# Two more units of an expert layer by nested Strassen products, with their transposed sums turned by DMA and VectorE

## Chip, cores and metric

The kernel runs on one core of a Trainium2 chip. The metric is the device time of one execution in microseconds, as the median over runs. The engines are TensorE (PE in the profile, its weight loads PEld), VectorE (DVE), ScalarE (ACT), GpSimd (POOL) and SyncE (SP, whose queue issues most DMAs).

## The reference

All data are float32. The attention comes first, and its output, as 3072 tokens by 512 features, is the input of the expert layer. The change lies in the expert layer's second product.

```python
# attention: q, k, v (4, 8, 768, 64), lam (8,); blocks of 64 positions
for b in range(nb):
    intra = einsum('bhij,bhjd->bhid', einsum('bhic,bhjc->bhij', qb, kb) * Dmask, vb)
    inter = einsum('bhid,bhde->bhie', qb * lam_pow, kv_state)
    out[:, :, sl] = intra + inter
    kv_state = lam_block * kv_state + einsum('bhsd,bhse->bhde', kb * rev_pow, vb)
x = out.transpose(0, 2, 1, 3).reshape(3072, 512)
# experts: w1 (4, 512, 1024), w2 (4, 1024, 512), domain_probs (3072, 4)
p = domain_probs / (domain_probs.sum(-1, keepdims=True) + 1e-09)
for e in range(4):
    h = maximum(x @ w1[e], 0.0)
    out += p[:, e:e + 1] * (h @ w2[e])
```

## The kernel before

**Units.** The 3072 tokens are cut into three groups of 1024 (g = 0, 1, 2; `LAST` is 2). A unit is one group with one expert: `units` has twelve, 0 to 3 for group 0, 4 to 7 for group 1, 8 to 11 for group 2, experts in the order 0, 1, 2, 3. The main loop takes unit after unit and in each the seven products of one Strassen level (`M1` to `M7`). Into each of these it interleaves the second product of the present unit with the first product of the next (`ahead`). So one pass of a unit is seven products of eight steps each; a step is a few matmuls, and the counter `now[0]` counts steps.

**First product** (`first_product`, L974). Two Strassen levels: seven times seven products of 128 by 128 weights with 256 tokens, two matmuls each. Its output blocks `m` are hidden values, hidden features on partitions and tokens along the row. DVE adds each result out of PSUM to a block; ACT copies or applies the ReLU (L982, L986, L915).

**Second product, plain** (`second_product`, L1028), for groups 0 and 1: one Strassen level, 112 matmuls of the program in a unit. The hidden block is the stationary operand, so the result has tokens on partitions. DVE multiplies it with the gate, which is there one number per partition, and adds it into `acc` (L1046, L1042). After the last expert the rows go to the output. The weights come by `feed2` from `w2_sums` or from the input.

**Second product, nested** (`nested_product`, L1256), for group 2: two levels, 98 matmuls in a unit. Here the weight block is stationary and the result is transposed, output features on partitions and tokens along the row; it stays so in `sums`, one tile for each of the seven products, over all four experts. The gate is now a row: `gated` multiplies the hidden block on POOL with a gate that a DMA has spread over the partitions (`gate_bc`). `outer_sums` makes the four outer sums of hidden blocks: ACT copies a block into a PSUM bank (`bring`, L838, tile `hp`), and DVE subtracts out of it into `hT`. `inner_sums` makes the inner sums on POOL (tile `acc` or `hT`). In the last unit the seven `sums` are joined, turned to token rows by TensorE (`give`, `turn_end`) or by DVE in 32 by 32 blocks (`give_across`), and stored. The last unit's `PLAIN` product uses one level (L1191).

**Weights of the nested product.** `prepare_w2_ops(e)` loads `w2[e]` (`w2b`), makes outer and inner sums of it on POOL (`w2o`, `ops`) and stores seven operands to DRAM (`w2_ops`). It runs as "chores": closures that `pump` takes one at a time as a modelled POOL (`busy`, with 480 elements of a row per step) comes free. `store` puts the DMAs of a finished chore into a queue; `until` forces chores whose result is needed. Before, expert e's is prepared while unit 4 + e runs. `feed3` loads the operands, two inner ones at a time, into the six buffers of `w2t`.

**Order.** All engines' queues are written out by hand: what a step appends stands in each engine's queue in that order. `background` holds DVE work and `aside` POOL work; a step takes one of each. `attention(g)` places the next groups' attention at steps given by `BEGIN`, eight chunks a fixed number of steps apart, and `x_fill` reads its result back as operands of the first product. All elementwise work goes through the helper `tt`, so that its line is L102 for DVE and POOL alike, and the tile names tell the groups apart. All DMAs that the text speaks of, but for the gates, are issued from SP's queue.

Of the kernel before, what the change touches and what calls it, by code (L numbers as in the profile page):

```python
# [21 lines left out]
def kernel(  # L22
# [78 lines left out]
    def tt(eng, o, a, b, op):  # L101
        eng.tensor_tensor(out=o, in0=a, in1=b, op=op)  # L102
        if eng is nc.gpsimd:
            busy[0] = max(busy[0], now[0]) + math.prod(o.shape[1:]) / 480
        else:
            vector(math.prod(o.shape[1:]), PSUM in (a.space, b.space))
# [6 lines left out]
    now, busy, free, filled = [0], [0.0], [0.0], [0.0]  # L113
# [7 lines left out]
    LAST = NG - 1  # L121

# [56 lines left out]
    def pump(pace=1.0, force=False):  # L179
        all_added(None if force else now[0])  # L180
        while results:
            results.pop(0)()
        while late and (force or late[0][0] <= now[0]):
            late.pop(0)[1]()
        begins = chores and (force or free[0] <= now[0])
        while queue and (force or queue[0][0] <= now[0] or begins and len(queue) > LEFT):
            queue.pop(0)[1]()
        if begins:
            begin = free[0] = max(free[0], now[0] - 1)
            was = max(busy[0], now[0])  # L190
            chores.pop(0)()
            free[0] = max(free[0], begin + max(pace * (busy[0] - was), 1))
# [106 lines left out]
    def inner_w2(e, m, blk):  # L299
        b = {f"A{i + 1}{j + 1}": blk[:, j, :, i * P:(i + 1) * P] for i in range(2) for j in range(2)}  # L300
        s = stage.tile([P, 4, 2, P], FP32, name="ops", tag="st")
        for name, x, y, op in S_OPS:
            b[name] = s[:, SLOT[name]]
            tt(nc.gpsimd, b[name], b[x], b[y], op)
        to = w2_ops[e, MS.index(m)]
        store(lambda: (
            nc.sync.dma_start(out=to[:, 0], in_=b["A11"]),
            nc.sync.dma_start(out=to[:, 1:3], in_=s[:, 0:2]),
            nc.sync.dma_start(out=to[:, 3], in_=b["A22"]),
            nc.sync.dma_start(out=to[:, 4], in_=b["S1"]),  # L310
            nc.sync.dma_start(out=to[:, 5], in_=b["A12"]),
            nc.sync.dma_start(out=to[:, 6], in_=b["S4"]),
            made.add(("w2", e, m)),
        ))

    def prepare_w2_ops(e):
        st = {}

        def block(name, i, j):
            t = stage.tile([P, 2, 2, DH], FP32, name="w2b", tag="st")  # L320
            src = moe_w2[e, j * W:(j + 1) * W, i * DH:(i + 1) * DH]
            nc.sync.dma_start(out=t[:].rearrange("p q c d -> p (q c) d"), in_=src.rearrange("(k p) d -> p k d", p=P))
            st[name] = t

        def total(name, a, b, op):
            t = stage.tile([P, 2, 2, DH], FP32, name="w2o", tag="st")
            halves(*(x[:].rearrange("p q c d -> p q (c d)") for x in (t, st[a], st[b])), op)
            st[name] = t

        return weight_steps(block, total, lambda m: inner_w2(e, m, st[A_OF[m]]))  # L330
# [164 lines left out]
    last_gate = consts.tile([P, CPG * E], FP32, name="last_gate")  # L495


    gate_rows = dram.tile([CPG, E, P], FP32, name="gate_rows")
    gate_bc = decay[:]

    def gates():
# [8 lines left out]
        for i in range(CPG):  # L510
            t = token(LAST, i // 4, i % 4) // P
            nc.vector.tensor_copy(out=last_gate[:, i * E:(i + 1) * E], in_=gate[:, t])

    def turn_gates():
        p, o = bank("s0", "gp"), small("gr")
        n = CPG * E
        nc.tensor.transpose(out=p[0:n, 0:P], in_=last_gate[:], identity=ident[:])
        nc.scalar.copy(out=o[0:n, 0:P], in_=p[0:n, 0:P])
        nc.scalar.dma_start(out=gate_rows[:].rearrange("n e p -> (n e) p"), in_=o[0:n, 0:P])
# [231 lines left out]
    BEGIN = {1: (24, 13), 2: (8 * 19, 22)}  # L751
    steps = []

    def attention(g):
# [4 lines left out]
        for i in range(CPG):  # L759
# [8 lines left out]
            if n == 2 * CPG + 3:  # L768
                put(s + 17, turn_gates)
# [41 lines left out]
    outer = {e: {n: {} for n in ("B11", "B12", "B21", "B22", "T1", "T2", "T3", "T4")} for e in range(E)}  # L811
# [43 lines left out]
    EARLY = E - 1, "M3"  # L855
# [42 lines left out]
    def finished(g, e, m, blocks, new):  # L898

        def later(to, a, b, order, relu=False):  # L900
# [7 lines left out]
            def step(at):  # L908
                x = there[at]
                if g == LAST and at != order[-1]:  # L910
                    bring(order[order.index(at) + 1])
                o = to[at] if at in to else small("m" + at)
                tt(nc.vector, o[:], x[:], b[at][:], ALU.add)
                if relu:
                    nc.scalar.activation(out=o[:], in_=o[:], func=AF.Relu)  # L915
                    if g == LAST:
                        gated(e, 1, 1, at, o)
# [4 lines left out]
            if g == LAST:  # L922
                background.append(lambda: bring(order[0]))
            background.extend(lambda at=at: step(at) for at in order)

        def keep(c, i, j):
            if g == LAST:
                outer_sums(e, *{(0, 1): (("T1",), ("T3", "T2")), (1, 0): (("T4",),)}.get((i, j), ()))
# [21 lines left out]
    def first_product(g, e, m, blocks, tags):  # L950
# [16 lines left out]
        def inner(i):  # L967
# [17 lines left out]
            if m in OUT and (at == "12" or not begins):  # L985
                nc.scalar.activation(out=new[at][:], in_=new[at][:], func=AF.Relu)  # L986
                if g == LAST:
                    gated(e, *OUT[m], at, new[at])
# [24 lines left out]
    def second_product(g, e, m, banks):  # L1013

        def part(sj, s):
# [31 lines left out]
            if e == E - 1 and m in ("M2", "M6", "M5", "M3"):  # L1047
                results.append(lambda: nc.sync.dma_start(out=rows[n][:, j * DH:(j + 1) * DH], in_=o))
# [10 lines left out]

    SEQ3 = ("M1", "M3", "M5", "M7", "M6", "M2", "M4")  # L1060
# [3 lines left out]
    def feed3(e, m, k):  # L1064

        until(("w2", e, m))
        if e == E - 1 and m != SEQ3[0]:

            if k == 0:
                t = xp.tile([P, 7, 256], FP32, name="w2s", tag="x" + SEQ[SEQ3.index(m)])  # L1070
                if (e, m) == PLAIN:
                    i, j = int(A_OF[m][1]) - 1, int(A_OF[m][2]) - 1
                    src = moe_w2[e, j * W:(j + 1) * W, i * DH:(i + 1) * DH]
# [3 lines left out]
                nc.sync.dma_start(out=t[:], in_=w2_ops[e, MS.index(m)].rearrange("p k c d -> p k (c d)"))  # L1077
# [6 lines left out]
            out=t[:, 0:n], in_=w2_ops[e, MS.index(m), :, 2 * k:2 * k + n].rearrange("p k c d -> p k (c d)"),  # L1084
# [97 lines left out]
    PLAIN = E - 1, "M2"  # L1182
# [23 lines left out]
    END = E - 1, SEQ3[-1]  # L1206
# [28 lines left out]

    def nested_product(e, m, tags):
        if e == 0:
# [8 lines left out]
        def inner(x, i):  # L1246
# [16 lines left out]
            if begins and e == 0:  # L1263
# [7 lines left out]
        def done():  # L1271
            if e == E - 1:
                to_join(m)

# [178 lines left out]
    units = [(g, e) for g in range(NG) for e in range(E)]  # L1453
    fill = [(*u, m) for u in units[2:] for m in SEQ]
    fill2 = [(*u, m) for u in units[:-E] for m in SEQ2]
# [51 lines left out]
    fill3 = [(e, m, k) for e in range(E) for m in SEQ3 for k in range(4)]  # L1507
# [6 lines left out]
    PACE = 1.0, 1.4, 1.0  # L1514
    for at, (g, e) in enumerate(units):
# [3 lines left out]
        nested, nests = g == LAST, ahead and ahead[0] == LAST  # L1519
        if g == LAST - 1:  # L1520
            chores.extend(prepare_w2_ops(e))
        if at == 6:
            forget()
        blocks, banks = {}, {}
        for i in range(7):
            if fill2:
                feed2(*fill2.pop(0))
            if (g, e) < (LAST, 0):
# [5 lines left out]
            if nests and i == 2:  # L1534
                nc.scalar.dma_start(
                    out=gate_bc, in_=gate_rows[:, ahead[1]].partition_broadcast(P),
                )
            if nested:
                pair = (at * 7 + i) % 2 if ahead else i % 3
                b = nested_product(e, SEQ3[i], (("q01", "q02"), ("q11", "q12"), ("g1", "g3"))[pair])  # L1540
                if i < 6 and (e, SEQ3[i + 1]) != PLAIN:
                    inner_sums(e, SEQ3[i + 1])
            else:
                b = second_product(g, e, SEQ2[i], banks)
            if nests and i == 6:
                inner_sums(ahead[1], SEQ3[0], nested)
                if ahead[1] == EARLY[0]:
# [4 lines left out]
            if nested and (e, SEQ3[i]) == END:  # L1552
# [9 lines left out]
            for x, part in enumerate(order):  # L1562
# [15 lines left out]
                if nested or nests:  # L1578
                    take(aside)
                if nested and ahead and x in (1, 3) and fill3:  # L1580
# [47 lines left out]
```

## Time and profile before

| | before |
|---|---|
| runs shown | 1170.91, 1176.38, 1176.42 us (median 1176.38) |
| profiled execution | 1171.55 us, its span 1169.8 us |
| PE busy, weight loads busy | 1157.8 us (99%), 1006.5 us (86%) |
| DVE, ACT, POOL busy | 791.7, 271.1, 646.1 us |
| granted PE clock | 1.0 throughout |
| DMA | 255.63 MB moved, mean 219 GB/s |

The span goes from the first to the last instruction; 1.75 us of the execution lie around it. The attention of group 0 and the start take the first 86 us, then come the units: plain ones to about 864 us, where the first nested product starts, and nested ones to the end. A trace row of a 128x256 matmul counts two for each matmul of the program. In the groups of the profile the form `out<-in` gives tile names, then shapes, the count, the sum and mean of the busy time, and the idle time just before with what ended it.

### The profile page before, as it was taken

Reading aid. Unit: us, or ns where it says so; the run is one execution under the profiler, and the core shown is the slowest. Engines: PE = TensorE matmul, PEld = TensorE weight load, DVE = VectorE, ACT = ScalarE, POOL = GpSimd, SP = SyncE. Lnnn points to the kernel's source line nnn. Section 1 sums busy time; section 2 is a strip of 40 time slices with the busy share of each in tenths; the row PEclk is TensorE's granted clock in tenths of the full one; section 3 lists DMA queues with packets and bytes.
Section 4 is the critical chain, followed back from the end, with each engine's and each line's share of the span. In section 5 each row is a group of like instructions: output and inputs, shape, how many; then the busy total and the mean of one; then the engine's idle time right before and its main releaser. Section 6 shows DMA issues by size and latency. Waiting matters only on the chain.

```text
span 1169.8 us, 21185 instructions
## 1 busy us (share of the span) xinstructions
PE 1157.8 (99%) x8095; PEld 1006.5 (86%) x8095; DVE 791.7 (68%) x1407; ACT 271.1 (23%) x540; POOL 646.1 (55%) x640
## 2 busy tenths in 40 slices
PE   8999999999999999999999999999999999999998
PEld 7888888888888888888888888888888888888887
DVE  4666895578478567657747836745775666777785
ACT  4321122112211201211211120221233342341231
POOL 2846327546655761065245215655893683882884
PEclk9999999999999999999999999999999999999999
DMA  9884668998997996787868757785765445354442
GB/s 208 219 257 153 185 195 264 289 315 255 310 334 228 311 277 188 221 264 230 247 195 261 243 182 239 215 278 184 252 212 194 140 152 181 129 182 148 154 180 73
DMA packets 265717, 255.63 MB, mean 219 GB/s; under 512 B 121328, under 2 KB 219408, under 8 KB 265616
## 3 DMA queue, kind: packets, MB, share of 16 engines
q1 hardware_dynamic: 254976, 251.46, 69.0%
q10 hardware_dynamic: 10640, 2.82, 1.1%
q8 instruction: 64, 1.05, 0.4%
q14 instruction: 37, 0.30, 0.1%
HBM read 180.80 MB, written 77.61 MB: 221 GB/s over the span
## 4 chain that ended last, share of the span: by engine, by line
PE 95%; DVE 3%; POOL 1%; issue 0%; DMA 0%; ACTq 0%; ACT 0%; POOLq 0%; DVEq 0%
PE pg L974 39%; PE q L1028 31%; PE pq L1256 13%; PE pM L1358 2%; PE pc L1358 2%; DVE m L102 1%; PE sp L633 1%; PE op L687 1%; PE op L705 1%; PE sp L640 1%; PE qp L603 1%; PE kp L603 1%; POOL acc L102 1%; POOL m L102 1%; DVE sums L102 0%
## 5 line engine op out<-in xcount | busy, mean ns | idle before, releaser
L974 PE MATMUL pg<-xs,ws_in 128*128 128x256 f32 x1960 | 471.6, 380 | 0.8 <-DVE m L102 0.7
L1028 PE MATMUL q<-w2t,m 128*128 128x256 f32 x1792 | 424.4, 380 | 0.0
L974 PEld LDWEIGHTS pg<-xs,ws_in 128*128 128x128 f32 x1960 | 369.8, 190 | 53.7 <-DVE m L102 3.3
L102 DVE TENSOR_TENSOR m<-pg,m 128x512 f32<-128x512 f32 x451 | 307.2, 687 | 120.0 <-PE pg L974 109.8
L1028 PEld LDWEIGHTS q<-w2t,m 128*128 128x128 f32 x1792 | 339.3, 190 | 46.6 <-DVE m L102 0.4
L1046 DVE SCALAR_TENSOR_TENSOR acc<-q,gate,acc 128x256 f32<-128x256 f32 x192 | 92.3, 481 | 126.2 <-PE q L1028 125.7
L102 DVE TENSOR_TENSOR m<-m,m 128x512 f32<-128x512 f32 x184 | 152.5, 829 | 7.7 <-ACT m L986 7.7
L986 ACT ACTIVATE m<-m 128x512 f32<-128x512 f32 x132 | 83.0, 630 | 303.6 <-DVE m L102 302.5
L102 POOL TENSOR_TENSOR m<-m,decay 128x512 f32<-128x512 f32 x64 | 81.8, 1293 | 58.1 <-ACT m L986 44.7
L102 DVE TENSOR_TENSOR sums<-pq,sums 128x256 f32<-128x256 f32 x153 | 64.1, 421 | 45.7 <-PE pq L1256 36.9
L982 ACT COPY m<-pg 128x512 f32<-128x512 f32 x88 | 51.5, 585 | 186.1 <-PE pg L974 176.1
L1256 PE MATMUL pq<-acc,w2t 128*128 128x256 f32 x352 | 86.6, 379 | 0.0
L102 POOL TENSOR_TENSOR xs<-xs 128x256 f32<-128x256 f32 x56 | 44.5, 794 | 73.1 <-DMA xs<-x_blocks 57.4
L1256 PEld LDWEIGHTS pq<-acc,w2t 128*128 128x128 f32 x352 | 66.8, 190 | 9.3 <-issue 0.3
L102 POOL TENSOR_TENSOR to<-xc 128x256 f32<-128x256 f32 x16 | 12.5, 783 | 95.8 <-DVE xc L102 67.8
L102 POOL TENSOR_TENSOR acc<-hT,hT 128x512 f32<-128x512 f32 x32 | 40.2, 1269 | 29.7 <-PE pq L1256 27.8
L102 POOL TENSOR_TENSOR kn<-kn,decay 128x512 f32<-128x512 f32 x16 | 18.0, 1123 | 64.6 <-PE kp L603 43.7
L102 POOL TENSOR_TENSOR w2o<-w2b 128x512 f32<-128x512 f32 x32 | 42.4, 1348 | 18.3 <-DMA w2b<-in_moe_w_dram 10.2
L915 ACT ACTIVATE m<-m 128x512 f32<-128x512 f32 x44 | 27.7, 630 | 106.8 <-DVE m L102 106.8
L102 POOL TENSOR_TENSOR ops<-w2b 128x256 f32<-128x256 f32 x24 | 17.8, 764 | 50.7 <-issue 28.2
L102 POOL TENSOR_TENSOR acc<-hT,acc 128x512 f32<-128x512 f32 x32 | 40.7, 1271 | 7.4 <-PE pq L1256 5.4
L102 POOL TENSOR_TENSOR w2o<-w2b,w2o 128x512 f32<-128x512 f32 x24 | 34.2, 1449 | 5.8 <-issue 4.3
(135 smaller groups left out, 1204.8 us busy)
## 6 DMA issues: line engine op xcount, KB each, us to landing
ws_in<-w_ops SPq DMA_DIRECT2D x70, 896.0 KB, 6.3
w2t<-w_ops SPq DMA_DIRECT2D x66, 256.0 KB, 5.1
w2t<-w_sums SPq DMA_DIRECT2D x64, 256.0 KB, 3.7
w_ops<-ops SPq DMA_DIRECT2D x28, 512.0 KB, 4.3
w2t<-in_moe_w_dram SPq DMA_DIRECT2D x48, 256.0 KB, 3.6
w2b<-in_moe_w_dram SPq DMA_DIRECT2D x32, 256.0 KB, 5.5
w_sums<-w2o SPq DMA_DIRECT2D x16, 512.0 KB, 5.7
w2b<-in_moe_w_dram SPq DMA_DIRECT2D x16, 512.0 KB, 7.6
```

The source lines that it names most:

```text
L102: eng.tensor_tensor(out=o, in0=a, in1=b, op=op)
L603: nc.tensor.transpose(out=x[:, ac * C:(ac + 1) * C], in_=y[:, 2 * ac:2 * ac + 2].rearrange("p r d -> p (r d)"), identity=ident[:],)
L633: nc.tensor.matmul(out=sp[r][half[x], ac * BL:(ac + 1) * BL], lhsT=hc(kT)[half[r], ac, blk[x]], rhs=hc(qT)[half[r], ac, blk[x]], start=(ac ...
L640: nc.tensor.matmul(out=sp[x][half[r], 256 + ac * D:256 + (ac + 1) * D], lhsT=kd[half[x], 2 * ac + r], rhs=vn[half[x], 4 * r + ac], start=F ...
L915: nc.scalar.activation(out=o[:], in_=o[:], func=AF.Relu)
L974: nc.tensor.matmul(out=p[:, j * 256:(j + 1) * 256], lhsT=ws[i][:, j * P:(j + 1) * P], rhs=xs[i], start=(fresh and j == 0), stop=True, skip ...
L982: nc.scalar.copy(out=new[at][:], in_=p[:])
L986: nc.scalar.activation(out=new[at][:], in_=new[at][:], func=AF.Relu)
L1028: nc.tensor.matmul(out=p[:, s * DH:(s + 1) * DH], lhsT=h[A_OF[m]][:, c * 256 + s * P:c * 256 + (s + 1) * P], rhs=fed2[g, e, m][uu][:, c], ...
L1046: nc.vector.scalar_tensor_tensor(out=o, in0=x, scalar=w, in1=o, op0=ALU.mult, op1=ALU.add)
L1256: nc.tensor.matmul(out=p[:, 0:256], lhsT=fed3[e, m, x // 2][:, x % 2, c * P:(c + 1) * P], rhs=b[B_OF[i]][:, c * 256:(c + 1) * 256], start= ...
L1358: nc.tensor.matmul(out=p[:, s * 256:(s + 1) * 256], lhsT=a[c][:, f:f + P], rhs=b[:, c, j * 256:(j + 1) * 256], start=(s == 0 and c == 0 an ...
```

## The change

Units 6 and 7 (group 1 with experts 2 and 3) get the nested second product as well. `NEST` = 6 is the first nested unit. The last group's experts now run in the order 2, 3, 0, 1, so that `w2_ops` of experts 2 and 3, prepared during units 4 and 5, serve units 6 and 7 and then 8 and 9; experts 0 and 1 are prepared during units 7 and 8 by a variant (`eased`) with smaller tiles and another order of its steps. From unit 7 on (`spare`) the model of POOL reckons 640 elements a step, a chore begins only if the modelled POOL is less than a step behind, and chores lie at least 3.2 steps apart. Attention of the last group is placed 16 steps apart instead of 22.

Group 1's experts 0 and 1 still add token rows into `acc`, which are now stored to a DRAM tensor `partial`. The transposed `sums` of units 6 and 7 are joined during unit 7 (`first_done`), ten additions of halves on DVE and four on POOL, and stored to the DRAM tensor `parked`. For each of the eight token tiles, four DMAs bring the 32 by 32 blocks of `parked` to the place where they belong after the turn and one DMA brings the rows of `partial` (`gather`); at least six steps later DVE turns all blocks of the tile (`turn_rows`), and at least two steps after that POOL adds the rows (`finish_rows`), which are then stored. `end_first` takes one such piece of work at a step.

The core of the diff:

```diff
@@ tt
-            busy[0] = max(busy[0], now[0]) + math.prod(o.shape[1:]) / 480
+            busy[0] = max(busy[0], now[0]) + math.prod(o.shape[1:]) / (640 if spare else 480)
@@ after LAST
+    units = [(g, e) for g in range(NG) for e in ((2, 3, 0, 1) if g == LAST else range(E))]
+    unit_of = {u: x for x, u in enumerate(units)}
+    NEST = 2 * E - 2
+    FINAL = len(units) - 1
@@ pump
-        begins = chores and (force or free[0] <= now[0])
+        begins = chores and (force or free[0] <= now[0] and not (spare and busy[0] > now[0] + 1))
...
-            free[0] = max(free[0], begin + max(pace * (busy[0] - was), 1))
+            free[0] = max(free[0], begin + max(pace * (busy[0] - was), 3.2 if spare else 1))
@@ prepare_w2_ops
-        return weight_steps(block, total, lambda m: inner_w2(e, m, st[A_OF[m]]))
+        def ready(m):
+            inner_w2(e, m, st[A_OF[m]], two)
+
+        if not eased:
+            return weight_steps(block, total, ready)
...
+        return [
+            lambda: (block("A21", 1, 0), block("A22", 1, 1)), pause(6),
+            lambda: total("S1", "A21", "A22", ALU.add),
+            lambda: (ready("M4"), block("A11", 0, 0), drop("A22")), pause(4),
+            less, lambda: ready("M7"), lambda: (ready("M1"), drop("S3")), lambda: ready("M5"),
+            lambda: (total("S2", "S1", "A11", ALU.subtract), block("A12", 0, 1)), lambda: ready("M6"),
+            lambda: ready("M2"),
+            lambda: total("S4", "A12", "S2", ALU.subtract), lambda: ready("M3"),
+        ]
@@ attention
-    BEGIN = {1: (24, 13), 2: (8 * 19, 22)}
+    BEGIN = {1: (24, 13), 2: (8 * 19, 16)}
@@ second_product
-            if e == E - 1 and m in ("M2", "M6", "M5", "M3"):
-                results.append(lambda: nc.sync.dma_start(out=rows[n][:, j * DH:(j + 1) * DH], in_=o))
+            if unit_of[g, e] in (E - 1, NEST - 1) and m in ("M2", "M6", "M5", "M3"):
+                to = rows[n] if g == 0 else partial[n % CPG * P:(n % CPG + 1) * P]
+                results.append(lambda: nc.sync.dma_start(out=to[:, j * DH:(j + 1) * DH], in_=o))
@@ before nested_product
+    ending, ended, gathered_out = [], [0], {}
+    parked = dram.tile([DOUT, G], FP32, name="parked")
+
+    def end_first(force=False):
+        if ending and (force or ended[0] + ending[0][1] <= now[0]):
+            ending.pop(0)[2]()
+            ended[0] = now[0]
+
+    def first_done(m):
...
+        def gather(n):
+            t, po = small("y"), small("po")
+            for b in range(4):
+                c = n * P + b * 32
+                nc.sync.dma_start(
+                    out=t[b * 32:(b + 1) * 32].rearrange("p (r c) -> p r c", c=32),
+                    in_=parked[:, c:c + 32].rearrange("(r p) c -> p r c", p=32),
+                )
+            nc.sync.dma_start(out=po[:], in_=partial[n * P:(n + 1) * P])
+            gathered_out[n] = t, po
+
+        def turn_rows(n):
+            t = gathered_out[n][0]
+            nc.vector.transpose(out=t[:], in_=t[:])
+            vector(W, False)
+
+        def finish_rows(n):
+            t, po = gathered_out.pop(n)
+            tt(nc.gpsimd, t[:], t[:], po[:], ALU.add)
+            store(lambda: nc.sync.dma_start(out=rows[CPG + n], in_=t[:]))
...
+        if m == "M4":
+            then(1, ("M4",), lambda: park("M4"))
+            order = 4, 5, 6, 7, 0, 1, 2, 3
+            for n in order:
+                then(6, (), lambda n=n: gather(n))
+                then(6, (), lambda n=n: turn_rows(n))
+                then(2, (), lambda n=n: finish_rows(n))
@@ main loop
+    PREPARED = {NEST - 2: 2, NEST - 1: 3, NEST + 1: 0, NEST + 2: 1}
...
-        nested, nests = g == LAST, ahead and ahead[0] == LAST
-        if g == LAST - 1:
-            chores.extend(prepare_w2_ops(e))
-        if at == 6:
+        nested, nests = at >= NEST, ahead and at + 1 >= NEST
+        if at in PREPARED:
+            chores.extend(prepare_w2_ops(PREPARED[at], nested))
+        if at == NEST + 1:
+            spare.append(True)
+        if at == NEST - 1:
             forget()
...
+                if ending and fits():
+                    end_first()
```

The rest of the diff replaces tests for the last group by tests for a nested unit, and indexes `outer`, `sums` and the fed weights by the unit's number.

## Prediction

> **What bounds the kernel now.** I read the page's busy table, its slices, the chain and the costliest groups, then PE's timeline, then windows by stage.
>
> ```profile
> PE 1157.8 (99%) x8095; PEld 1006.5 (86%) x8095; DVE 791.7 (68%) x1407; ACT 271.1 (23%) x540; POOL 646.1 (55%) x640
> ...
> PE   8999999999999999999999999999999999999998
> ...
> PE 95%; DVE 3%; POOL 1%; issue 0%; DMA 0%; ACTq 0%; ACT 0%; POOLq 0%; DVEq 0%
> ...
> L1028 PE MATMUL q<-w2t,m 128*128 128x256 f32 x1792 | 424.4, 380 | 0.0
> ```
>
> PE is busy in every slice and the chain is PE for 95%: matmuls taken away shorten the run, unless something else becomes late. Their price is not the mean of 380 ns, because matmuls overlap, but the distance of their starts, in PE's timeline:
>
> ```profile
> 930.41 1.89 PE L974 MATMUL pg<-xs,ws_in 128*128 128x256 f32 x8
> 932.14 1.03 PE L1256 MATMUL pq<-acc,w2t 128*128 128x256 f32 x4
> 933.00 1.03 PE L1256 MATMUL pq<-m,w2t 128*128 128x256 f32 x4
> ```
>
> 932.14 - 930.41 = 1.73 us for 8, so 0.216 us each. The trace has two for each matmul of the program (1792 for 896), so a program matmul costs 0.432 us.
>
> The windows of the last plain stage and of three nested units show the room on the other engines (columns after the length: PE, PEld, DVE, ACT, POOL busy, clock, DMA share, GB/s):
>
> ```profile
> 762.00:866.00 104.00, 103.39 (x477) 90.10 (x476) 67.23 (x107) 23.71 (x41) 69.17 (x71) 1.00 0.73 235
> 866.00:951.00 85.00, 85.00 (x396) 74.74 (x394) 50.71 (x88) 34.09 (x72) 56.74 (x46) 1.00 0.50 164
> 951.00:1036.00 85.00, 85.00 (x395) 74.62 (x394) 62.14 (x116) 25.52 (x45) 55.55 (x45) 1.00 0.46 158
> 1036.00:1120.00 84.00, 83.97 (x389) 73.62 (x389) 61.06 (x114) 25.03 (x44) 55.06 (x45) 1.00 0.51 177
> ```
>
> A nested unit takes 85 us of PE and 55 to 57 of POOL; nearly 30 us of POOL are free. There is one place where a late POOL has already reached PE, at the step into the nested units: first ACT's line, then DVE's.
>
> ```profile
> 859.89 0.59 ACT L838 COPY hp<-m 128x512 f32<-128x512 f32 x1 [7.18 <-POOL m L102]
> ```
> ```profile
> 860.52 0.69 DVE L102 TENSOR_TENSOR hT<-hp,m 128x512 f32<-128x512 f32 x1 [1.97 <-ACT hp L838]
> ```
>
> ACT waited 7.18 us for a gated block of POOL; its copy held DVE for 1.97 us, behind which the evacuations of PE's banks stood in the queue. PE's starts then slipped by about 1.0 us (862.84 to 863.09, and another 0.8 at its first nested product). So about 1 to 1.5 us of lateness is absorbed, the rest is PE's. In a nested unit the same copy has no room left: the gate of 952.27 ended at 953.5, and the copy that needs it started at 953.61.
>
> [...]between 848.7 and 854.7, four such DVE adds (m<-m,m) took 1.08 to 1.36 us (mean of the form 0.83), and POOL's 128x512 multiplies up to 1.71 (minimum 1.27). [...]L585 turns 128x512 in 0.70 us after DMAs had put each 32x32 block in its place.
>
> **The change part by part.**
> PE: 224 plain matmuls go, 196 nested ones come, 28 fewer: 28 x 0.432 = **-12.1 us**. The transposition adds no matmul; turning 64 rows of gates instead of 32 is still one. All of this lies on the path.
>
> ACT: +24 hp x 0.59, +28 sums x 0.37, +16 up x 0.59 = +34 us on 271; hidden under PE, ACT stays below a third.
>
> DVE: removed 56 x 0.48 (acc) and 48 x 0.83 (m<-m,m); added 32 hT x 0.68, 16 m<-up x 0.68, 70 sums x 0.42, 10 whole sums x 0.83, 8 transposes x 0.70, 8 gate copies x 0.16: -66.7 + 77.4 = +11 us on 792. Hidden as a sum; by product the fullest are the last two of unit 7, with 13.0 and 13.2 us for 12.1 of PE: some 2 us late there at most.
>
> POOL: 100 instructions of 128x512 more (56 inner sums, 32 gates, 8 final adds, 4 sums; w2's differences keep their number) x 1.28 = +128 us, to 774. They all fall into the nested units, together with the preparation of two experts' w2, which stood in the plain units 6 and 7 and now stands in units 7 to 10. I count POOL's instructions in the order of the loop's steps, at 1.28 us for 128x512 and 0.78 for 128x256. Unit by unit that is 72, 73, 85, 87 and 63 us for units 6 to 10, against 84.7 of PE; the same count for units 9 and 10 of before gives 56.3, where the trace has 55.5. Units 8 and 9 are fuller than PE's time. By product (12.1 us of PE) the excess adds up from the last product of unit 8 on: 15.4, 13.4, 9.0, 12.6, 12.1, 13.4, 13.4, 12.8, 13.4. The backlog is 4.6 us after the first product of unit 9 and 6.6 after the first of unit 10; elsewhere it peaks at 4.3 in the middle of unit 8, where no hp copy needs it, and at 2.0 at its start. With 1.5 us absorbed at each start of a unit: 0.5 (unit 8) + 3.1 (unit 9), and at unit 10, where PE's lost 3.1 were POOL's gain, 6.6 - 3.1 - 1.5 = 2.0. Sum **+5.6 us**. Its bounds: 0, if POOL finds its inputs earlier than my count by steps lets it; 12, if contention makes its instructions 1.35 us (w2o rows: 1.35 and 1.45), which adds 5% of 109 us in the full stretch.
>
> SP: 970 to 1066 instructions. The new ones are the stores of partial and parked (20), the gathers (32 of 64 KB, and 8 of po), the split loads of w2b, and more w2t. A DMA occupies SP for 0.4 to 0.6 us, and the fullest product (unit 9, the fourth) has 25, some 12 us: no room for a wait. Loads of w2t and ws_in stand in that queue behind stores which wait for POOL (at most 5.4 us before, L213). I take this at 0, covered by the loads' one product of lead; its upper bound is the second rival's.
>
> DVE's new wait: each transpose comes at least six steps (9.1 us) after its gather. Five issues at 0.6 and a landing like that of the nearest row (across, also 128-byte pieces: 2.1 to 9.9, median 5.1) make 8.1 us: in time by 1.0. PE waits for what stands behind the transpose.
>
> Moved: attention of the last group is 16 steps apart instead of 22. It adds no work; DMA share there rises from 0.81, DVE to at most 14.8 us for 13 in one product. I take 0, bounds -1 (it clears the step into the nested units) to +3. The expert order of the last group and FINAL rename what is last; the tail is the same work: 0.
>
> Sum: -12.1 + 5.6 = **-6.5 us**. Against the profiled execution (1171.55, span 1169.8) that is 1165.0. The three runs shown go from 1170.91 to 1176.42 with the median 4.8 above the profiled one; the changed kernel should scatter alike, 1165 to 1170, and I name **1167**.
>
> **The rivals.**
> *All hidden*: POOL runs ahead of my count. -12.1 alone: 1159.5 to 1164. For it: 56 us of 85 before, with no loss of PE in three units, and chores that wait for DMAs rather than for PE. Against: hp had no room at 953.6.
> *POOL eats it*: bound of 12 above, 1171.5 to 1175, no change. For it: [...]transposes and whole sums just where POOL is full; against: they are 18 instructions.
> *Gathers hold DVE* (slower): in each of eight transposes DVE waits for the last of four gathers, behind a held SP. At the slowest landing of the nearest row, 9.9 + 3.0 = 12.9 us, it is 3.8 late, 2.3 of it PE's: 8 x 2.3 = 18.4, so 1171.55 - 12.1 + 5.6 + 18.4 = 1183.5. It decides the sign's size when the mean lateness passes 3.1 us (landing 12.2 us after the gather's step). For it: 25 issues in one product. Against: DMA share is 0.46 to 0.51 in these units.
> *The change doesn't do what it says*: excluded for PE by the count of 28; the turn through DMA is in the program's order too.
>
> **How the numbers follow.** A measurement of this kernel can tell about 0.5% (5.9 us) from no change. Chances: my forecast 0.36, all hidden 0.18, POOL eats it 0.26, gathers 0.20. The first lies just across the border, so 0.30 of its 0.36 count as faster: faster 0.48, same 0.32, slower 0.20. The likeliest case's own range is 1162 to 1172; the whole reaches from 1159 (all hidden) to 1182, near the gathers' case.
>
> **What would show it.** The nested rows (pq) grow by 392 in the trace and the plain ones (q) fall by 448; POOL is busy 765 to 790 us; PE is idle for a few us at the starts of units 9 and 10, with ACT hp waiting for POOL m. Wrong: DVE's transpose waiting for a DMA by more than 3 us, PE idle for w2t or ws_in, or no PE idle at all.

## The result, and the profile after

| | before | after |
|---|---|---|
| median of the runs (lowest to highest) | 1173.13 us (1170.91 to 1176.9), 11 runs | 1180.6 us (1175.47 to 1188.07), 11 runs |
| profiled execution, its span | 1171.55, 1169.8 us | 1177.99, 1176.2 us |
| granted PE clock, mean | 1.0 | 0.996 |

The change makes the kernel slower: the ratio of after to before, on one chip, is 1.0062, with an interval of 1.0037 to 1.0086. I had forecast 1167 us with a range of 1159 to 1182; the median lies in the range, on the wrong side of the kernel before.

From the page of the kernel after, the busy table, PE's slices, the chain by engine and two of the costliest groups:

```profile
PE 1153.4 (98%) x8039; PEld 998.4 (85%) x8039; DVE 798.6 (68%) x1447; ACT 301.8 (26%) x608; POOL 763.2 (65%) x740
...
PE   8999999999999999999999999999998999999998
PEclk9999999999999999999999999999998999999999
...
PE 88%; DVE 4%; DMA 3%; POOL 3%; issue 1%; SPq 1%; ACT 0%; ACTq 0%; POOLq 0%; DVEq 0%
...
L1060 PE MATMUL q<-w2t,m 128*128 128x256 f32 x1344 | 318.7, 380 | 0.5 <-DVE m L102 0.5
...
L1367 PE MATMUL pq<-acc,w2t 128*128 128x256 f32 x576 | 143.4, 382 | 5.2 <-DMA w2t<-w_ops 4.6
```

PE has the 56 trace matmuls less that I counted: 8095 to 8039, with plain `q` down by 448 and the nested groups up by 392. ACT grew as worked out (to 301.8 us), POOL a little less (to 763.2 us; 774 forecast). What is new: the chain is PE for 88% instead of 95%, DMA has 3% of it instead of 0%, one slice of PE and of its clock has fallen to 8, and the nested matmuls of inner sums have 4.6 us of idle time before them that ended with the landing of `w2t`. The slice is the one around 890 us; PE's timeline there (start, duration, form, count, and in brackets the idle time before it and what ended it):

```profile
886.54 1.89 PE L1367 MATMUL pq<-acc,w2t 128*128 128x256 f32 x8
888.27 1.89 PE L1006 MATMUL pg<-xs,ws_in 128*128 128x256 f32 x8
894.25 2.04 PE L1367 MATMUL pq<-acc,w2t 128*128 128x256 f32 x4 [4.08 <-DMA w2t<-w_ops]
896.08 1.91 PE L1367 MATMUL pq<-hT,w2t 128*128 128x256 f32 x4
897.79 2.94 PE L1006 MATMUL pg<-xs,ws_in 128*128 128x256 f32 x8
```

PE stands still for 4.08 us, and afterwards the same matmuls have twice the distance: four of them take from 894.25 to 896.08, 0.46 us each instead of 0.216. The windows say why (length, then PE, PEld, DVE, ACT, POOL busy, clock, DMA share, GB/s):

```profile
888.00:894.00 6.00, 2.16 (x11) 1.55 (x9) 1.81 (x3) 0.00 (x0) 5.76 (x8) 0.92 1.08 361
894.00:897.00 3.00, 2.75 (x7) 2.25 (x8) 0.42 (x1) 0.00 (x0) 2.84 (x5) 0.50 1.00 402
897.00:900.00 3.00, 3.00 (x9) 2.37 (x8) 0.68 (x2) 0.00 (x0) 3.00 (x3) 0.51 1.23 274
900.00:903.00 3.00, 3.00 (x16) 2.64 (x15) 1.57 (x3) 0.86 (x2) 2.84 (x4) 1.00 1.01 309
```

In the trace's record of the clock it is half from 893.1 to 899.9 us, for 5.7 us after PE had gone on. The idle time cost a second time, as slow matmuls: 2.87 us by the measure given below.

Who was late is read from SP's timeline, the queue that issues these loads:

```profile
877.70 0.37 SPq L312 DMA_DIRECT2D w_ops<-w2o  x1
882.38 0.33 SPq L312 DMA_DIRECT2D w_ops<-ops  x1
882.76 1.41 SPq L312 DMA_DIRECT2D w_ops<-w2o  x1
884.22 0.46 SPq L312 DMA_DIRECT2D w_ops<-ops  x1
884.73 0.46 SPq L312 DMA_DIRECT2D w_ops<-w2o  x1
885.28 0.47 SPq L312 DMA_DIRECT2D w_ops<-ops  x1
885.79 0.46 SPq L1291 DMA_DIRECT2D parked<-sums  x1
886.36 1.11 SPq L330 DMA_DIRECT2D w2b<-in_moe_w_dram  x2
889.26 0.82 SPq L1118 DMA_DIRECT2D w2t<-w_ops  x2
```

The store of prepared weights (`w_ops`, L312) at 882.38 begins 4.3 us after the DMA ahead of it ended, and SP's waits say for whom:

```profile
SPq L312 <- POOL ops L102: 14.0, 4, 4.6
```

That is 14.0 us in four waits, the longest 4.6, from 668 to 1060 us. SP was waiting for POOL to finish an inner sum of w2. Behind it, in order, stood four more such stores, one of `parked`, two loads of `w2b`, and only then, at 889.26, the `w2t` that PE wanted at 890.2 and began to use at 894.25.

Two more things stand in the trace at this place. Ahead of the `w2t` SP waited once more, from 887.5 to 889.2 us, for the landing of the store issued at 882.76. In the trace the DMAs of SP and ACT count up eight semaphores in turn, and each issue ended only after the eighth DMA before it had landed (all 805 for which the trace has that landing, 0.32 us or more after it). This store, landed at 889.20, was the eighth before the `w2t` of 889.26:

```profile
SPq L1118 <- DMA w_ops<-w2o: 1.7, 1, 1.7
```

And in the third product of every unit from unit 5 on ACT's queue issues the load of the next unit's gates (`decay` is the tile; 512 KB, spread over the partitions). In the view of the DMA queues from 884 to 888 us (packets, MB, share), q10 is this load and q1 holds what SP issues:

```profile
q10 hardware_dynamic: 973, 0.49, 43.1%
q1 hardware_dynamic: 122, 0.07, 5.8%
```

While the gates were moved SP's stores hardly were; then, from 888 to 904 us, the DMA engines were full (share 1.08).

To compare kernels I use one measure of loss, worked out from PE's timeline: the distance of starts beyond 0.216 us for each 128x256 trace matmul, summed from 600 us to the end. It is -0.8 us for the kernel before, so good to about 1 us, and 14.6 for the kernel after. It comes from the one profiled execution of each kernel, which is not always a typical one; so the medians of the runs are set beside it. The main terms of the 14.6: 4.25 of idle time and 2.87 at half clock around 890; 2.15 between 845 and 860 (PE waits for DVE's `m`); 2.61 at 1000; 0.66 at 932 (again `w2t`); the rest in pieces below 1 us. The piece at 1000 has a DMA behind it too, in DVE's timeline:

```profile
999.69 0.69 DVE L102 TENSOR_TENSOR m<-up,m 128x512 f32<-128x512 f32 x1 [4.10 <-DMA w_ops<-ops]
```

DVE could not write a block because an earlier content of its memory, inner sums of w2, was still being stored; PE got its bank back 2.46 us late. In the part before, from 86 to 600 us, the loss is 6.5 against 5.2, so the closer placing of the attention seems to have cost 1.3 us. From the first to the last matmul of the plain second product the kernel before takes 594.5 us, the kernel after 595.4, and its eleven variants below that have the same program there up to 598.0: the cost is known only as some 1 to 3 us.

### The profile page after: what moved, and what is told of

Same layout as the page of the kernel before. It is cut to its first block, busy times and chain, and to the rows that moved or that the text cites. A ratio compares the mean times of both kernels' runs of the same rounds, so it can differ in the third digit from the quotient of the medians.

```text
span 1176.2 us, 21570 instructions
## 1 busy us (share of the span) xinstructions
PE 1153.4 (98%) x8039; PEld 998.4 (85%) x8039; DVE 798.6 (68%) x1447; ACT 301.8 (26%) x608; POOL 763.2 (65%) x740
## 4 chain that ended last, share of the span: by engine, by line
PE 88%; DVE 4%; DMA 3%; POOL 3%; issue 1%; SPq 1%; ACT 0%; ACTq 0%; POOLq 0%; DVEq 0%
PE pg L1006 36%; PE q L1060 24%; PE pq L1367 17%; PE pM L1471 3%; DMA w2t<-w_ops 2%; PE pc L1471 2%; DVE m L102 2%; PE sp L665 1%; POOL m L102 1%; PE op L719 1%; DVE sums L102 1%; PE op L737 1%; POOL acc L102 1%; PE sp L672 1%; PE qp L635 1%
## 5 line engine op out<-in xcount | busy, mean ns | idle before, releaser
L1060 PE MATMUL q<-w2t,m 128*128 128x256 f32 x1344 | 318.7, 380 | 0.5 <-DVE m L102 0.5
L1060 PEld LDWEIGHTS q<-w2t,m 128*128 128x128 f32 x1344 | 254.1, 190 | 35.7 <-DVE m L102 1.2
L102 POOL TENSOR_TENSOR m<-m,decay 128x512 f32<-128x512 f32 x96 | 122.3, 1294 | 41.8 <-ACT m L1018 34.1
L1367 PE MATMUL pq<-acc,w2t 128*128 128x256 f32 x576 | 143.4, 382 | 5.2 <-DMA w2t<-w_ops 4.6
L102 DVE TENSOR_TENSOR sums<-pq,sums 128x256 f32<-128x256 f32 x223 | 92.6, 421 | 69.8 <-PE pq L1367 62.2
L1367 PEld LDWEIGHTS pq<-acc,w2t 128*128 128x128 f32 x576 | 109.4, 191 | 22.3 <-issue 6.3
L102 DVE TENSOR_TENSOR m<-m,m 128x512 f32<-128x512 f32 x136 | 114.0, 838 | 4.2 <-ACT m L1018 4.2
L1367 PE MATMUL pq<-hT,w2t 128*128 128x256 f32 x240 | 62.7, 384 | 2.5 <-DVE sums L102 2.5
L102 POOL TENSOR_TENSOR kn<-kn,decay 128x512 f32<-128x512 f32 x16 | 18.5, 1159 | 67.6 <-PE kp L635 47.2
L1367 PEld LDWEIGHTS pq<-hT,w2t 128*128 128x128 f32 x240 | 45.9, 192 | 9.6 <-DVE sums L102 2.9
L870 ACT COPY hp<-m 128x512 f32<-128x512 f32 x72 | 41.5, 589 | 44.7 <-POOL m L102 24.8
```

Of the source, the lines that this page charges most:

```text
L870: nc.scalar.copy(out=there[x][:], in_=blk[at][:])
L1060: nc.tensor.matmul(out=p[:, s * DH:(s + 1) * DH], lhsT=h[A_OF[m]][:, c * 256 + s * P:c * 256 + (s + 1) * P], rhs=fed2[g, e, m][uu][:, c], ...
L1367: nc.tensor.matmul(out=p[:, 0:256], lhsT=fed3[e, m, x // 2][:, x % 2, c * P:(c + 1) * P], rhs=b[B_OF[i]][:, c * 256:(c + 1) * 256], start= ...
```

## The experiments

**Theories.** A (what the trace suggests): SP's queue. The stores of the prepared weights, with their waits for POOL and their bytes, stand ahead of the loads that PE needs; the gathers add to it. B (my forecast): POOL's sums themselves are late, and hidden blocks with them. C (the rival of the prediction): the gathers and what waits for them hold DVE or SP.

The verdicts are ratios to the kernel before on the same chip in the same session. Where a kernel prepares nothing for experts 0 and 1, units 10 and 11 read the operands of experts 2 and 3 in their place.

### e1: without the preparation of experts 0 and 1

```diff
-    PREPARED = {NEST - 2: 2, NEST - 1: 3, NEST + 1: 0, NEST + 2: 1}
+    PREPARED = {NEST - 2: 2, NEST - 1: 3}
```

> The preparation of w2 of experts 0 and 1 inside the nested units is left out; units 10 and 11 read the operands of experts 2 and 3, with the same DMAs and matmuls. Its 65 us of POOL and its loads and stores on SP's queue vanish. Theory SP (weight loads stand in SP's queue behind the preparation's stores): the losses at 889, 931 and 996 us go with the dip of the clock, some 11 us of the changed kernel's 15; about 1166 against the 1178 of its profiled execution. Theory POOL (full POOL makes hp copies and inner sums late): the same 11 us and more go. Theory DVE (the final additions of whole sums at 843 to 860 and the transposes hold DVE): nearly all stays, 1175 or more.

Measured: 1167.51 us (1163.55 to 1174.31), ratio 0.9931 (0.9908 to 0.9953), loss 0.5. Nearly all the loss is gone, so it needs the preparation, its POOL work or its DMAs; the rest of the change by itself (gathers, transposes, whole sums, token rows) costs PE about 1 us. The ratio is worth 8.1 us of the 12.1; this remainder and the attention's 1 to 3 us account for most of the difference, so the price of PE's part is borne out.

### e2: the sums are made, but not stored

```diff
-        store(lambda: ([nc.sync.dma_start(out=to[:, x], in_=b[n]) for n, x in at], ...
+        if e > 1:
+            store(lambda: ([nc.sync.dma_start(out=to[:, x], in_=b[n]) for n, x in at], ...
```

> The sums of the preparation of experts 0 and 1 are still made on POOL, but their 84 stores are left out (units 10 and 11 read the operands of experts 2 and 3). POOL's work is that of the changed kernel, SP's queue is relieved. Theory SP: as without any preparation, 1165 to 1168, no clock dip. Theory POOL: the losses stay, 1174 to 1178, with PE waiting for POOL or for hp.

Measured: 1168.3 us (1164.39 to 1172.36), ratio 0.9942 (0.9924 to 0.9959), loss 2.9. PE's waits from 600 us on (sum, times, longest), the whole list:

```profile
PE pg L1007 <- DVE m L102: 2.3, 6, 1.0
PE q L1061 <- DVE m L102: 0.5, 1, 0.5
PE yp L1188 <- DVE sums L102: 0.3, 1, 0.3
PE pg L1369 <- DVE sums L102: 0.3, 1, 0.3
PE pq L1369 <- POOL acc L102: 0.2, 1, 0.2
```

No wait for `w2t` is left, with POOL's sums all still there. So the 84 stores carry 14.6 - 2.9 = 11.7 us of the loss (by the ratios of the runs, 1.0062 and 0.9942, some 14 us), and POOL's work for the preparation 2.9 - 0.5 = 2.4 us. The second figure rests on two profiled executions; the runs of e1 and e2 can't be told apart. Most of the 2.4 us (1.8) stand at 848 to 861, where DVE joins whole sums: with POOL's sums beside them ten of these adds take 1.31 us each in the mean (1309 ns here), without them (e1) 1.16.

```profile
L102 DVE TENSOR_TENSOR sums<-sums 128x512 f32<-128x512 f32 x10 | 13.0, 1309 | 0.1
```

### e3: loads and stores kept, POOL's sums left out

```diff
+            if e > 1:
                 tt(nc.gpsimd, b[name], b[x], b[y], op)
+            else:
+                b[name] = b["A11"]
...
-            for q in range(2):
-                tt(nc.gpsimd, b[q], a[q], b[q], ALU.subtract)
```

> The loads and stores of the preparation of experts 0 and 1 stay in number and size, but POOL makes no sums for them; the stores take loaded blocks and so no longer wait for POOL (units 10 and 11 read the operands of experts 2 and 3). If it is the number of issues on SP and the traffic: 1174 to 1178, w2t still late. If it is the wait of stores for POOL with w2t behind them, or POOL itself: 1165 to 1169.

Measured: 1172.24 us (1168.23 to 1178.02), ratio 0.9982 (0.9963 to 1.0), loss 6.5. PE's largest wait:

```profile
PE pq L1372 <- DMA w2t<-w_ops: 4.8, 3, 2.6
```

With the same bytes and as many stores, but none that waits for POOL's sums, `w2t` is still late, three times, by 2.6 at most. The clock did not fall. So SP's waits for POOL are not needed for a late `w2t`, though less is lost without them: neither expectation holds. The edit also moves things: the model of POOL no longer fills, so the chores come sooner, with 90 DMA issues on SP between 863 and 935 us instead of 82 and a DMA share of 0.93 in unit 8 instead of 0.80. The part that is left, 6.5, is that of a denser crowd.

### e10: 84 stores of 512 bytes each

```diff
+        else:
+            store(lambda: ([nc.sync.dma_start(out=to[:, x]...[0:1, 0:128], in_=b[n][0:1, 0]) ...
```

> Each of the 84 stores of prepared operands of experts 0 and 1 is still issued, at its place and with its waits, but moves 512 bytes of one partition instead of 128 to 256 KB (units 10 and 11 read the operands of experts 2 and 3). If issues and the waits in SP's queue alone hold w2t: as the changed kernel, 1178 to 1181. If it is the bytes and the time to land, which keep the eight DMAs in flight longer: as without stores, 1167 to 1170.

Measured: 1173.82 us (1170.12 to 1179.84), ratio 1.0001 (0.9987 to 1.0016), loss 9.8. The idle time at 890 stays, with its half clock; the ones at 932 and 1000 are gone.

```profile
893.89 2.04 PE L1371 MATMUL pq<-acc,w2t 128*128 128x256 f32 x4 [3.15 <-DMA w2t<-w_ops]
```

So of the 11.7 us about 14.6 - 9.8 = 4.8 go with the bytes, and 9.8 - 2.9 = 6.9 stay with 84 issues of next to nothing (by the ratios some 7 us each). The 6.9 are not all time in SP's queue. At 890 us SP was ahead of the kernel after by 3.2 us:

```profile
886.02 1.27 SPq L1122 DMA_DIRECT2D w2t<-w_ops  x2
```

Yet PE went on at 893.89, nearly as late as in the kernel after: the loads took 7.7 us to land instead of 4.9. The load of the gates was on its way until 891.6, and two loads of `w2b` stood ahead.

### e11: without the gathers

```diff
-            for b in range(4):
-                ...
-                nc.sync.dma_start(out=t[b * 32:(b + 1) * 32]..., in_=parked[:, c:c + 32]...)
...
-            nc.vector.transpose(out=t[:], in_=t[:])
```

> The turn of the transposed sums is left out: no gathers of parked, no transposes on DVE, no final adds on POOL; the rows of partial are stored alone, so units 6 and 7 do not reach the output of the middle group. If gathers hold DVE or crowd SP's queue: 4 to 8 us less than the changed kernel, 1173 to 1177. If the preparation's stores alone decide: 1177 to 1181.

Measured: 1174.21 us (1172.43 to 1181.03), ratio 1.0013 (0.9999 to 1.0028), loss 9.7. `w2t` is still late by 4.7 us at 890; the late one at 932 is gone, and at 1000 a loss of 1.1 us is left, now for `w2t`. The gathers and what follows them carry some 5 us, and not by DVE: in the kernel after none of the transposes waited for a DMA. They begin only after the first late `w2t`, so they are not its cause. That they act through SP is argued, not shown: there the four issues of the first tile take 4.76 us:

```profile
892.73 4.76 SPq L1297 DMA_DIRECT2D y<-parked  x4
```

### e5: gathers issued from ACT

```diff
-                nc.sync.dma_start(
+                nc.scalar.dma_start(
...
-            nc.sync.dma_start(out=po[:], in_=partial[n * P:(n + 1) * P])
+            nc.scalar.dma_start(out=po[:], in_=partial[n * P:(n + 1) * P])
```

> The whole computation; the 40 loads of the gathers are issued from ACT's queue instead of SP's, all else as in the changed kernel. If SP's many issues hold w2t, the losses where gathers stand ahead of w2t (931 and 996 us) go and the first at 889 us, where no gather is ahead, stays: 2 to 5 us less, 1176 to 1179 in the median against 1180.6. If the gathers hold DVE by their landing, nothing changes.

Measured: 1180.42 us (1176.09 to 1187.47), ratio 1.0047 (1.0031 to 1.0063), loss 14.6: nothing gained. `w2t` at 890 is late by 3.8 us, the one at 932 is in time, and the loss goes to ACT. From ACT's timeline:

```profile
953.00 3.27 ACTq L1301 DMA_DIRECT2D po<-partial  x1
956.30 1.07 ACT L1014 COPY m<-pg 128x512 f32<-128x512 f32 x2 [4.84 <-DMA y<-parked]
```

ACT stood 4.84 us at the issues of a gather instead of emptying PE's bank. So the time of the issues was taken here from an engine that computes.

### e6, e7 and e8: later stores, wider spacing, and a bundle

```diff
# e6
-        queue.append((busy[0] + 2, f))
+        queue.append((busy[0] + (5 if spare else 2), f))
# e7
-            free[0] = max(free[0], begin + max(pace * (busy[0] - was), 3.2 if spare else 1))
+            free[0] = max(free[0], begin + max(pace * (busy[0] - was), 6 if spare else 1))
# e8: the edits of e5 and e7, and
-        at = (("A11", 0), ("S3", slice(1, 3)), ("A22", 3), ("S1", 4), ("A12", 5), ("S4", 6))
+        at = (("A11", 0), ("S3", slice(1, 3)), ("A22", 3), ("S1S4", slice(4, 7, 2)), ("A12", 5))
```

> The whole computation; from unit 7 on a store of prepared operands is issued five modelled steps after POOL should be done with it instead of two. The number of issues is the same. If it is the store's wait for POOL that holds w2t behind it, the loss of 4.25 us at 889 us and the dip of the clock after it go: median 1170 to 1174. If it is the number of issues, 1178 to 1182. Tiles are held longer, so DVE may wait for a store's landing more often (2.6 us at 996 us before).

> The whole computation; from unit 7 on chores lie at least 6 steps apart instead of 3.2, so that POOL's fullest unit falls from 87 to some 77 us and the issues on SP are spread to unit 10 (their fullest product still has 19). If the crowd of issues and waits on SP decides: 1168 to 1173. If the number over the whole stage decides, 1178 or more.

> The whole computation; gathers from ACT's queue, chores 6 steps apart, and two of a store's six DMAs merged into one. By the theory that SP's queue is what ate the gain, this comes near the run without stores: 1166 to 1170, about 0.6% below before. By the theory that POOL's or DVE's load bounds it, it stays above 1173.

Measured: e6 1180.83 us (1179.06 to 1185.69), ratio 1.0048 (1.0025 to 1.0072), loss 20.7. e7 1172.9 us (1169.64 to 1178.79), ratio 0.9991 (0.9976 to 1.0007), loss 7.0. e8 1185.37 us (1178.36 to 1187.27), ratio 1.0077 (1.0039 to 1.0115), loss 19.0.

Asking for a store three steps later does not help: by the runs e6 can't be told from the kernel after (its profiled execution, with a loss of 20.7, is the slowest of its eight). The stores hardly wait for POOL's inner sums there, 1.7 us in all between 668 and 1060 us instead of 14.0, and yet `w2t` is 5.3 us late at 890. What SP waited for ahead of it was the landing of the gates' load. PE's wait in e6, and SP's:

```profile
PE pq L1367 <- DMA w2t<-w_ops: 10.0, 2, 5.3
SPq L330 <- DMA decay<-gate_rows: 4.7, 1, 4.7
```

Setting chores wider apart (e7) takes half of the loss away; what is left is 2.5 us of late `w2t` and 1.4 us of PE waiting for POOL's `acc` in the last units, since the preparation now ends later. The bundle loses the gain of e7: ACT is held at the gathers (6.3 us of PE's waits), and a `w2t` is late by 3.1 us. Moving an issue a few steps or to another engine is no cure by itself; a thinner stage helps.

### e4: all preparation early, in the plain units

```diff
-    PACE = 1.0, 1.4, 1.0
+    PACE = 1.0, 1.0, 1.0
-    PREPARED = {NEST - 2: 2, NEST - 1: 3, NEST + 1: 0, NEST + 2: 1}
+    PREPARED = {1: 2, 2: 3, 3: 0, 4: 1}
```

> The whole computation; all four experts' w2 operands are prepared in the plain units (entered at units 1 to 4 instead of 4, 5, 7 and 8) and chores of the middle group are paced 1.0 instead of 1.4, so that they end before the first nested unit. Theories SP and POOL: the nested units lose only DVE's 2 us and the start's, 1165 to 1168; the fullest product in the plain units then has 32 issues on SP in 13 us, which may cost up to 4 us there. Theory DVE: 1175 or more.

Measured: 1193.06 us (1188.51 to 1194.61), ratio 1.0149 (1.0104 to 1.0194). From 600 us on the loss is 2.9, but from 90 us on it is 35.1. PE's timeline in the plain units:

```profile
508.48 3.75 PE L1006 MATMUL pg<-xs,ws_in 128*128 128x256 f32 x8 [6.92 <-DMA ws_in<-w_ops]
535.23 3.75 PE L1006 MATMUL pg<-xs,ws_in 128*128 128x256 f32 x8 [9.60 <-DMA ws_in<-w_ops]
```

The plain units prepare by the variant with the larger tiles. The nested units are relieved, and the same queue fails earlier, with the loads of the first product's weights (`ws_in`) in place of `w2t`. Eight matmuls here take 3.75 us instead of 1.9: half clock again (0.50 from 508.5 to 511.5 us and from 535.0 to 538.0). PE stood there while the DMA engines were busy: their share was 0.79 from 499.0 to 508.5 us and 0.90 from 524.0 to 535.0. The nested units are not the only ones without room for the preparation; SP's queue, and the DMA engines behind it, lack it in the plain units too.

### e9 and e12: the preparation spread over units 6 to 9

```diff
# e12; e9 has the merged store of e8 besides
-    PREPARED = {NEST - 2: 2, NEST - 1: 3, NEST + 1: 0, NEST + 2: 1}
+    PREPARED = {NEST - 2: 2, NEST - 1: 3, NEST: 0, NEST + 1: 1}
...
+        if at == NEST:
+            spare.append(3.9)
         if at == NEST + 1:
-            spare.append(True)
+            spare.append(7)
...
-            ... 3.2 if spare else 1))
+            ... spare[-1] if spare else 1))
```

> The whole computation; the preparation of experts 0 and 1 begins at unit 6 instead of 7, chores lie 3.9 steps apart in unit 6 and 7 steps from unit 7 on, and two of a store's six DMAs are merged. SP then has at most 16 issues in a product of the nested units (25 in the changed kernel, 19 at 6 steps) and POOL at most 16 us. By the theory that the crowd on SP's queue decides: 1165 to 1170, 0.3 to 0.8% below before. If the merged and earlier preparation only moves the crowd: 1172 or more.

> The whole computation; the preparation begun at unit 6 and spread as in e9_even, but with six DMAs for each store as in the changed kernel. If spreading alone frees SP's queue: within 2 us of e9_even, 1165 to 1169. If the merged DMA was needed: 1170 to 1173, with w2t late around 890 to 910 us as at 6 steps.

Measured: e9 1165.94 us (1164.34 to 1170.58), ratio 0.9943 (0.9921 to 0.9965), loss 1.4. e12 1166.35 us (1162.93 to 1171.03), ratio 0.992 (0.9891 to 0.9949), loss 2.5. PE's waits from 600 us on in e9, the two largest:

```profile
PE pg L1006 <- DVE m L102: 0.9, 3, 0.4
PE pq L1367 <- DMA w2t<-w_ops: 0.6, 2, 0.5
```

The work is the same as in the kernel after, and all of it is done. Begun a unit earlier and set wider apart, it leaves SP 57 issues from 863 to 935 us in e9 (59 in e12) where the kernel after has 82 and e2, without stores, 49 (counted in SP's timeline). SP's stores still wait for POOL's inner sums, 12.6 us in ten waits in e9, and the gates' load of unit 8 takes 11.0 us to land instead of 5.5; with fewer issues around them PE hardly notices. Nor is it the mean load of the DMA engines: their share in units 8 and 9 is 0.76 and 0.75 in e9, 0.80 and 0.81 in the kernel after, 0.63 and 0.64 in e10. Both versions beat both kernels: by 0.6 and 0.8% the kernel before, by over 1% the kernel after. Between the two the intervals overlap; the merged store is worth nothing that can be told. (The profiled execution of e9, 1170.58 us, is the slowest of its six: its first matmul of the plain second product comes 5.2 us later than in the trace of before.)

## Why the prediction was wrong

**PE's term, -12.1 us: right.** The counts came as worked out, and e12, with the whole change in it, gains 0.8% of its session's 1176.08 us, 9.4 us; e1 has a loss of 0.5 us.

**SP at 0: the step that failed.** I wrote "no room for a wait", saw stores that wait for POOL ahead of the loads, and took the term at 0, "covered by the loads' one product of lead". It measured 11.7 us in the stores (e2 against after), of which 2.87 are the clock. At 890 us the lead was used up by a 4.3 us wait for POOL, eight issues, a wait of 1.7 us for a landing, and 4.9 us until the load itself had landed. I had counted SP's DMAs in the fullest product, one of unit 9; the largest loss fell in the third product of unit 8, where stores of prepared weights, parked sums, loads of `w2b` and the load of the gates meet. The upper bound, put down as the second rival's, would have held it whichever rival is meant (12 us for POOL, 18.4 for the gathers); the value did not. I had also set the DMA share of before, 0.46 to 0.51, against the gathers; after the change it is 0.80 in these units.

**POOL's backlog, +5.6 us: right mechanism, wrong place and size.** The copies of hidden blocks did wait for POOL. ACT's group in the page of the kernel after, with its idle time last:

```profile
L870 ACT COPY hp<-m 128x512 f32<-128x512 f32 x72 | 41.5, 589 | 44.7 <-POOL m L102 24.8
```

24.8 us, against 7.2 before; but PE's waits for POOL come to 0.5 us in all. The absorption is larger than the 1.5 us at each start of a unit that I allowed. POOL cost 2.4 us by another way (e2 against e1, one execution each): with its sums beside them DVE's whole sums, which I had priced at 0.83 us, took 1.31 instead of 1.16. POOL's lateness mattered where I had not put it, at SP's stores.

**DVE at 0 as a sum** held over the run; by product it did not at 845 to 860 us (2.15 us), about the end of unit 7, whose last products I had named the fullest, with "some 2 us late there at most" that I did not count. **Attention**, at 0 with bounds of -1 and +3, measured +1.3, within the 1 to 3 us of the other traces.

**The rivals.** "Gathers hold DVE" has the right sign and a price near the mark, but its mechanism did not occur: no transpose waited. My range reached up to the result only for the sake of this case, so that it held is luck. The gathers are worth about 5 us (e11), through SP as it seems. "All hidden" is what e9 and e12 show for a better-spaced queue. "POOL eats it" fell: e2 has POOL as full and is faster, and the eight transposes took 0.70 us each, as priced.

**No term for the clock.** The half clock after a wait stood in no step. Part of the scatter of the kernel after (12.6 us over its runs, 6.0 for the kernel before) goes with it: the mean clock of a run lay between 0.989 in the slowest and 0.997 in the fastest. Of the sum: -12.1 for the matmuls, +15.4 for the loss from 600 us on (14.6 against -0.8) and +1.3 before it make +4.6; the spans differ by 6.4. The 1.8 us between them lie ahead of the units and can't be put down to the change: the first matmul of the plain second product starts at 86.4 us in the trace of before, at 89.0 in that of after, and between 85.1 and 92.6 in the traces of the experiments, whose program is the same as that of after up to there.

**What stays open.** That the stores make `w2t` late is shown by e2; how the time divides between SP's waits, its issues, the landings and the full DMA engines is not: waits (e3, e6), bytes (e10) and issues (e5, e11) were each lightened by themselves, and `w2t` stayed late around 890 us. The limit of eight DMAs in turn was not tried alone (the stores landed 1.8 to 8.5 us after issue, median 5.6). Nor was the load of the gates: in all eight traces in which PE stood over 1 us for `w2t` between 890 and 903 us, it was issued at 881 to 888 us and landed 2 to 7 us before PE went on. It is there in e1, e2, e9 and e12 as well, so by itself it does no harm; whether the stall would come without it is open.

## What to carry to other kernels

Count a DMA queue by stage as one counts an engine: its issues, the waits of each, and how many may be in flight. SP's issues stand in order in the trace, so the store that waited 4.3 us for POOL was a wait for every load behind it, and a prefetch covers only what its lead exceeds: at 890 us PE waited 4.08 us more. Moving work from this full queue to another engine's (e5) or a few steps later (e6) moved the stall; beginning one unit earlier and spreading evenly removed it but for losses of 1.4 us (e9) and 2.5 us (e12) in place of 14.6. Count DMAs of other queues that fall into the same stage too. And count the clock: after the waits of 3.11 us and more in the units, by my estimate from the windows, 1.7 to 3.0 us more were lost at half clock.

## What the runs showed of the hardware

The granted clock fell after short waits. In the units, idle times of PE of 3.11 (e8), 3.15 (e10), 3.81 (e5), 4.08 (after), 4.64 (e8), 4.67 (e11), 4.74 and 5.27 (e6), 6.92 and 9.60 us (e4) were each followed by a clock of 0.50 to 0.53 in the window of about 3 us behind them; those of 2.37 (e5), 2.46 (after, at 1000 us) and 2.63 us (e3) were followed by 1.00. Worked out from the clocks of the windows, the dips last 3.4 us (e5, e11, the first of e8), 6.8 us (after, e6, e10, the second of e8) or 10.2 us (e4), and end 3.4 to 6.1 us after PE goes on. I estimate the loss as half of the time at half clock after PE goes on, 1.7 to 3.0 us; for the 5.7 us of the kernel after the starts give 2.87. In e4, after the 6.92 us:

```profile
508.50:511.50 3.00, 3.00 (x7) 2.44 (x8) 0.00 (x0) 0.59 (x1) 0.00 (x0) 0.50 0.99 336
511.50:514.50 3.00, 3.00 (x10) 2.35 (x10) 0.00 (x0) 0.59 (x1) 0.00 (x0) 0.60 0.89 280
514.50:517.50 3.00, 3.00 (x16) 2.64 (x15) 1.95 (x3) 0.59 (x1) 2.55 (x3) 1.00 1.01 283
```

No limit between harmless and harmful waits is shown. Nothing was measured between 2.63 and 3.11 us, and the profile's ends of matmuls are modelled. Near the start of the kernel after, behind an idle time of 2.31 us, the clock was 0.51 from 15.8 to 19.3 us; in the kernel before, behind the same 2.31 us, it was 1.00. In the units I would keep below 2.6 us, the longest wait that went without a dip.

A second one: the mean of 0.83 us for DVE's adds of 128x512 with both inputs in SBUF (`m<-m,m` before) did not hold for the ten adds of whole sums: 1.16 us in the mean without the preparation's sums on POOL, 1.31 with them. Single ones of the kernel after lie between 0.68 and 1.79 us, with POOL busy for over 90% of each; so it is not POOL's being busy alone that sets the time.
